# Gated mix of segmented attention and a feed-forward layer: v of the first segment from unscaled float32r halves, and matmuls on zeros at the beginning

## The chip, the core and the metric

The kernel runs on one core of a Trainium2 chip. A core has a matrix engine (TensorE, PE in the profile, which writes into PSUM, eight banks of 128 x 512 float32), a vector engine (VectorE, DVE), a scalar engine (ScalarE, ACT), GpSimd (POOL) and SyncE (SP), which here issues every DMA. The engines run beside each other and wait for each other by semaphores; each takes its own instructions in the order of the program. The metric is the time of one execution on the device in microseconds. Before the change the median of three runs was 551.74 us (551.17 to 552.27).

## What is computed

Sixteen heads of 28 columns, four segments of 512 rows. Cut to what matters:

```python
def reference(A_x, A_wq, A_wk, A_wv, A_wo, A_beta, B_x, B_w1, B_w2, gate_w):
    # x: (1, 2048, 448); wq, wk, wv, wo: (448, 448); w1: (448, 1792); w2: (1792, 448)
    q, k, v = heads(x @ wq), heads(x @ wk), heads(x @ wv)      # 16 heads of 28
    M = z = 0
    for s in range(4):                                         # segments of 512 rows
        a_dot = softmax(q[s] @ k[s].T * 28 ** -0.5 + causal) @ v[s]
        a_mem = phi(q[s]) @ M / (phi(q[s]) @ z + 1e-6)         # phi(t) = t + 1 or exp(t)
        o[s] = sigmoid(beta) * a_mem + (1 - sigmoid(beta)) * a_dot
        M, z = M + phi(k[s]).T @ v[s], z + phi(k[s]).sum(rows)
    a = merge(o) @ wo
    b = silu(x @ w1) @ w2
    g = sigmoid((x * gate_w).sum(-1))
    return g * a + (1 - g) * b
```

## The kernel before

Products are made in split precision. An operand becomes two float16 halves, the rounded value and what the rounding left, and a product is three matmuls for each 128 rows of the contraction (high by high, low by high, high by low). The 448 rows are three blocks of 128 and one of 64, whose low half lies in the idle rows, so a product of 512 columns is 11 matmuls (`passes`, `product`, L532, which cuts it into four tasks, one for each block). So that float16 holds the values, each operand is first multiplied by a power of two, worked out on the chip: `size` (L381) takes the largest magnitude of a tile on VectorE, and `scales(a, b)` (L399) reduces those, transposes the column on TensorE (L418), reduces the row and rounds it to a power of two on VectorE (L421 to L425), spreads it to all partitions with a small matmul (L427) and stores it and its inverse in `top` and `up` (L431, L432). Only then can `halves` (L513) make the two halves: the high one on ScalarE (L516), the low one on VectorE (L508) or, in two instructions, on GpSimd (L510, L511).

The first stage (`project`, L675) loads x of segment 0 and the weights of v, q and k in this order on SP's queue (L954 to L977), derives their scales, and makes for each segment the projections q and k (`proj`, four groups of heads each, into the three "mm" banks) and v with the gate's column (`vproj`, four blocks of 128 rows, into the three "sc" banks), the memory's updates (`memory`) and retrievals (`retrieve`). phi(q) is kept in float32r halves (L836, L838), a 32-bit form that the matmul takes directly: its high half is a rounding copy, its low half a subtraction, and neither needs a scale. A projection leaves PSUM in two steps, the high half by ScalarE (L806, L862) and the low half by VectorE (L807, L866), goes to DRAM, and comes back for attention. After the stage attention (`attention`, L1160) runs for 16 groups of four heads, interleaved with the feed-forward layer (`unit`, L1051), and at the end the output projection (`last_part`).

Before the data is there TensorE runs 15 matmuls on a tile of zeros (`maskb`, L718); the tile becomes the causal mask later (L728, on GpSimd), which waits for them.

The order on every engine is made while the program is built, by a list planner (`Sched`, L118). Each piece of work is a task with an engine, a cost, dependencies, buffers and a priority, a number of which the smaller goes first. The planner always takes the task that can start earliest on its engine, and among those that can start at once the one with the smallest number; for TensorE it also weighs the loading of weights against it (`PRICE`). A task that may run on VectorE or GpSimd (`either`, `scaled`) goes to the one that can start it first, unless it would end more than `SLACK` later there than on the other; in the plan the two lock each other out while a task of that kind runs. So all constants at the top (L46 to L95) are priorities and parameters of this planner: QS and KS1 for the scales and halves of q's and k's weights, VC for v's scale of segment 0, XS0 for the sizes of x, VF, VA and VS for the blocks of v, LOP and PVP for the low halves of the probabilities and P·V, WOT and WOP for the tail. The plan only sets the order; on the chip each instruction starts when its engine and its semaphores allow.

Of the kernel before, what the change touches and what calls it, by code (L numbers as in the profile page):

```python
# [8 lines left out]
F32 = mybir.dt.float32  # L9
# [27 lines left out]
WARM = 15  # L37
# [9 lines left out]
WOT = -23.27  # L47
# [8 lines left out]
SLACK = 0.67  # L56
LOP = 33.77
LATE = 0.08
FIRST = 104.18
WPRIO = 134.65  # L60
# [4 lines left out]
MP = 34.45  # L65
VF = 0.02
VA = 1.68
VS = 15.54
NV = 8
XS0 = 16.16  # L70
VC = -4.07
OT1 = -16.51
XS = 17.15
QS = -15.23
KS1 = 15.74
SS = -13.76
XH0 = -8.84
XLD = -11.75
# [6 lines left out]
PRICE = 25.59  # L85
PVRUNS = [((1, 0), 1)]
PVP = 81.22
FLO = -69.24
FHI = 869.75
WOP = 155.66  # L90
SZ = 30.78
SZSTEP = 2.16
XPRIO = 171.43
WBP = -21.83
# [152 lines left out]
def infini_mix(ctx: ExitStack, tc: tile.TileContext, x, wq, wk, wv, wo, beta, w1, w2, out):  # L247
# [111 lines left out]
    tg = const.tile([128, NSEG], F32, name="tg")  # L359
    rv = const.tile([128, NSEG], F32, name="rv")  # L360
# [83 lines left out]
    def vscale(s, prio):  # L444
        VREADY[s] = dve(130, lambda: nc.vector.tensor_scalar(tg[:, s:s + 1], top[:, WG:WG + 1], top[:, xi(s)], -1.0,
                                                             op0=OP.mult, op1=OP.mult), SCALED[WG], SCALED[NSEG - 1 - s],
                        prio=prio)
# [65 lines left out]
    def halves(j, hi, lo, dst, src, n, d, prio, takes=(), uses=()):  # L513

        s = up[:, j:j + 1]
        h = copy(n + 110, lambda: nc.scalar.activation(dst()[hi], src(), AF.Copy, scale=s), d, SCALED[j], takes=takes,  # L516
# [9 lines left out]
    def x16(s, c, prio):  # L526
# [3 lines left out]
        XH[s, c] = halves(NSEG - 1 - s, (ALL, c), lo, lambda: X16[s], lambda: r.v, L, d, prio, uses=[r])  # L530
# [144 lines left out]
    def project():  # L675
        es = ExitStack()
        wp = es.enter_context(tc.tile_pool(name="pw", bufs=1))
        W = {n: wp.tile([128, 8, D + 2 if n == "v" else L], F16, name=f"w{n}s") for n in "qkv"}
# [29 lines left out]
        def c1():  # L708
# [9 lines left out]
        t_wb = pe(half(L, WARM), lambda: [nc.tensor.matmul(  # L718
            wb.v, maskb, maskb[:, None, :].to_broadcast([128, 4, 128]), start=True, stop=True) for _ in range(WARM)],
            t_wm, takes=[wb], prio=-200)  # L720
        END1.append(t_wb)
        t_on = dve(32, lambda: nc.vector.memset(ones, -TALL), prio=-50)
# [648 lines left out]
```

## Time and profile before

| | |
|---|---|
| median of 3 runs | 551.74 us (551.17 to 552.27) |
| the profiled execution: time, span | 553.39 us, 551.7 us |
| mean granted TensorE clock | 0.984 of full speed |
| busy of the span: TensorE, VectorE, ScalarE, GpSimd | 534.8, 409.3, 391.8, 354.7 us |
| first matmul that belongs to a product | at 16.85 us |
| last projection's matmul of v | ends near 155.1 us |

The profile is that of one execution; its span runs from the first to the last instruction. Lines are named L and a number, those of the listing above; a line can be that of a helper which many places call, and then the tiles tell them apart (`wvs`, `wqs`, `wks` are the halves of the weights, `xh` those of x, `raw` the weights as loaded, `xraw` x as loaded). `out<-in` gives the tile written and the tiles read. A TensorE instruction counts as busy from its start to a modelled end, at whatever clock was granted, so a busy stretch at half clock does half the work.

### The profile page before, as it was taken

How to read it: one execution, taken by the hardware profiler on the slowest of the kernel's cores; microseconds unless marked ns; L12 is line 12 of the kernel's file. 1: busy time of each engine (PE TensorE's matmuls, PEld its weight loads, DVE VectorE, ACT ScalarE, POOL GpSimd, SP SyncE). 2: the span in 40 equal slices, each digit the busy share in tenths (PEclk: the TensorE clock that was granted, in tenths of full speed). 3: DMA queues.
4: the chain of work that ended last, by engine and by line, in shares of the span. 5: the costliest groups of instructions: out<-in, count | busy, mean ns of one | idle time of the engine just before them, and what ended most of it. 6: DMA issues, size and time to landing. Idle time of an engine off the chain costs nothing.

```text
span 551.7 us, 11563 instructions
## 1 busy us (share of the span) xinstructions
PE 534.8 (97%) x4009; PEld 294.7 (53%) x4009; DVE 409.3 (74%) x1074; ACT 391.8 (71%) x688; POOL 354.7 (64%) x519
## 2 busy tenths in 40 slices
PE   4699999999999999999999999999999999999997
PEld 1234655655554556555665555655555555555444
DVE  6889999899789966777666779766987319646473
ACT  1588898986656977899877997878998896402140
POOL 2063254845830689988999987999999995213120
PEclk8689999999999999999999999999999999999999
DMA  8658998885586434312433234434301515698962
GB/s 276 205 175 227 203 236 233 225 226 166 170 233 162 146 100 137 87 42 80 121 102 102 58 98 124 121 103 112 100 18 53 138 49 152 219 241 212 225 160 83
DMA packets 89194, 81.68 MB, mean 148 GB/s; under 512 B 55176, under 2 KB 78856, under 8 KB 89136
## 3 DMA queue, kind: packets, MB, share of 16 engines
q1 hardware_dynamic: 89136, 80.95, 53.1%
q8 instruction: 31, 0.51, 0.4%
q14 instruction: 27, 0.22, 0.1%
HBM read 48.41 MB, written 26.09 MB: 135 GB/s over the span
## 4 chain that ended last, share of the span: by engine, by line
PE 89%; DVE 4%; DMA 4%; ACT 1%; issue 1%; SPq 0%; DVEq 0%; ACTq 0%
PE mm L540 31%; PE mm L1086 23%; PE sc L540 12%; PE sc L1182 6%; PE sc L644 6%; PE cc L1216 6%; DMA rawf<-in_w_dram 2%; PE cc L932 1%; DMA xraw<-in_x_dram 1%; PE cc L895 1%; DVE sizes L388 1%; DVE sc L654 1%; DMA v_scr<-vt 1%; PE sc L640 1%; PE cc L933 0%
## 5 line engine op out<-in xcount | busy, mean ns | idle before, releaser
L1203 POOL TENSOR_TENSOR phl<-pf,phl 128x384 f16<-128x384 f32 (+1 forms) x192 | 189.5, 1008 | 16.2 <-ACT phl L1199 16.2
L1086 PE MATMUL mm<-wb,ghl 128*128 128x448 f16 (+1 forms) x684 | 148.8, 349 | 0.0
L540 PE MATMUL mm<-xh,wa 128*128 128x512 f16 x572 | 141.4, 379 | 0.0
L1187 ACT ACTIVATE pf<-sc,es 128x512 f32<-128x512 f32 (+1 forms) x192 | 109.7, 623 | 19.8 <-PE sc L1182 18.6
L654 DVE CUSTOM_DVE_ANT_0 sc<-sc,mk 128x384 f32<-128x384 f32 (+1 forms) x192 | 104.8, 572 | 20.4 <-PE sc L644 19.1
L1086 PEld LDWEIGHTS <-ghl 128*128 128x128 f16 x684 | 65.0, 97 | 52.5 <-DVE ghl L508 0.3
L1199 ACT ACTIVATE phl<-pf 128x1280 f16<-128x1280 f32 x64 | 81.3, 1277 | 14.9 <-POOL pf L1193 14.9
L540 PEld LDWEIGHTS <-wa 128*128 128x128 f16 x572 | 53.6, 97 | 54.4 <-issue 1.4
L1182 PE MATMUL sc<-ring 86*128 86x512 f16 (+3 forms) x256 | 59.3, 299 | 0.4 <-ACT pf L1187 0.2
L644 PE MATMUL sc<-ring 84*128 84x128 f16 (+3 forms) x256 | 58.2, 299 | 0.1
L1224 DVE TENSOR_REDUCE oraw<-cc 128x116 f32<-128x232 f32 x64 | 25.3, 395 | 30.8 <-PE cc L1216 30.6
L1063 ACT ACTIVATE th<-mm,ths 128x512 f32<-128x512 f32 x52 | 35.8, 699 | 16.0 <-PE mm L540 15.8
L1216 PEld LDWEIGHTS <-phl 128*128 128x128 f16 x1280 | 41.9, 96 | 9.1
L540 PE MATMUL mm<-xh,wqs 128*128 128x512 f16 x176 | 44.5, 390 | 1.0 <-ACT wqs L516 0.7
L551 POOL TENSOR_TENSOR ol<-ol,ml 128x448 f32<-128x448 f32 x12 | 13.7, 1138 | 48.7 <-DMA ol<-o_scr 37.2
L1065 DVE SCALAR_TENSOR_TENSOR mm<-th,mm 128x512 f32<-128x512 f32 x52 | 35.7, 694 | 10.9 <-ACT th L1063 10.9
L1216 PE MATMUL cc<-vg,phl 128*128 128x29 f16 (+1 forms) x1280 | 43.6, 182 | 0.0
L540 PE MATMUL sc<-wvs,xh 128*128 128x450 f16 x176 | 39.9, 368 | 3.1 <-ACT wvs L516 2.1
L540 PE MATMUL mm<-xh,wks 128*128 128x512 f16 x176 | 42.1, 380 | 0.0
L1069 DVE SCALAR_TENSOR_TENSOR ghl<-mm,ghl 128x512 f16<-128x512 f32 x52 | 35.1, 683 | 5.6 <-ACT ghl L1067 5.2
L1182 PEld LDWEIGHTS <-ring 86*128 86x128 f16 x256 | 23.8, 97 | 22.0 <-issue 1.1
L1067 ACT ACTIVATE ghl<-mm 128x512 f16<-128x512 f32 x52 | 30.9, 604 | 6.5 <-DVE mm L1065 6.4
(165 smaller groups left out, 835.9 us busy)
## 6 DMA issues: line engine op xcount, KB each, us to landing
rawf<-in_w_dram SPq DMA_DIRECT2D x26, 256.0 KB
rawf<-in_w_dram SPq DMA_DIRECT2D x28, 224.0 KB
xraw<-in_x_dram SPq DMA_DIRECT2D x16, 256.0 KB
v_scr<-vt SPq DMA_DIRECT2D x16, 232.0 KB
vg<-v_scr SPq DMA_DIRECT2D x16, 232.0 KB
q_scr<-stg SPq DMA_DIRECT2D x16, 224.0 KB
ring<-q_scr SPq DMA_DIRECT2D x16, 224.0 KB
k_scr<-stg SPq DMA_DIRECT2D x16, 224.0 KB
```

Source lines behind the costliest of these rows:

```text
L540: nc.tensor.matmul(ps(), *p[i], start=(i == 0), stop=(i == n - 1))
L644: nc.tensor.matmul(ps.v[:, u:u + n], rg.v[:KS, 0, hh, i * 128:(i + 1) * 128], rg.v[:KS, 1, hh, :n], start=(i > 0), stop=(i > 0 or j == 3), ...
L654: nc.vector.tensor_tensor_reduce(r, r, MK[:, L - n:], 1.0, NEG, OP.add, OP.max, mx.v[:, hh, i:i + 1])
L1063: e1 = sact(L, lambda ps=ps, th=th: nc.scalar.activation(th.v, ps.v, AF.Tanh, scale=ths[:, s:s + 1]), m, DER[s], takes=[th], uses=[ps], pr ...
L1065: e2 = dve(L, lambda ps=ps, th=th: nc.vector.scalar_tensor_tensor(ps.v, th.v, 1.0, ps.v, op0=OP.add, op1=OP.mult), e1, uses=[ps, th], prio=p0)
L1069: e4 = dve(L, lambda ps=ps, g=g: nc.vector.scalar_tensor_tensor(g.v[:, 1], ps.v, DOWN, g.v[:, 0], op0=OP.mult, op1=OP.subtract), e3, uses= ...
L1086: nc.tensor.matmul(ps.v[:, lo:hi], g.v[:, y, sl], w.v[:, z, lo:hi], start=(j == 0 and i == 0), stop=(j == len(fs) - 1 and i == 2))
L1182: nc.tensor.matmul(ps.v[:, e:e + w], rg.v[:KK, 1, hh, j * 128:(j + 1) * 128], rg.v[:KK, 0, hh, j * 128:], start=True, stop=True)
L1187: ex.append(sact(e, lambda b=b, ps=ps, pf=pf, e=e: nc.scalar.activation(pf.v[:, b, :e], ps.v[:, :e], AF.Exp, scale=es[:, s:s + 1]), m, *ex ...
L1199: hi = copy(1280, lambda hl=hl, flat=flat: nc.scalar.activation(hl.v[:, 0], flat(), AF.Copy), *mk, takes=[hl], uses=[pf], prio=p0 + 2)
L1203: low = pool(w - u, lambda hl=hl, flat=flat, u=u, w=w: nc.gpsimd.tensor_sub(hl.v[:, 1, u:w], flat()[:, u:w], hl.v[:, 0, u:w]), low, uses=[ ...
L1216: nc.tensor.matmul(p[:, i, :2 - z], hl.v[:, z, u:u + 128], vg.v[:, j, hh, :2 - z], start=(z == zs[0] and i == 0), stop=(z == zs[-1] and j ...
```

## The change

v of segment 0 (four blocks, `vproj`) is computed from float32r halves of x and of wv, made from the loaded tiles without a scale. `full` makes them: a copy on ScalarE that rounds to float32r, and a subtraction on VectorE or GpSimd (new tiles `xr` and `wr`). The product is then too large by the two scales that x and wv would have had, so the copies out of PSUM multiply with `sv` = `up[wv] * up[x] * FIT` in place of the constant FIT, and the gate's column takes the factor -1 in place of `tg`. The float16 halves of x and wv are still made: x's for q and k, wv's for the later segments. They now wait for the float32r halves of the same tile.

The matmuls on zeros at the beginning become a task of 12 full ones, four rounds of four in tiles of 32 rows (28 used) and three rounds of two in tiles of 64 rows, each tile of a round into a bank of its own; behind it eight tasks of two full ones with the largest priority number, which the planner puts wherever TensorE has nothing else to start. The mask on GpSimd waits for the last of them.

Almost all priorities and planner parameters get new values; the order of segments 1 to 3, of attention, of the feed-forward layer and of the tail is thereby planned anew. Among them: v's scale (VC -4.07 to -1.35), v's weights' float16 halves (-8.6 to VH = 6.63), v's sizes (-8.9 to WSZ = -11.62), x's float16 halves (-8.8 to XQ = -13.14), q's scale and halves (QS -15.23 to -23.13), the second to fourth blocks of v of segment 0 (VA + VS k, from 17.2, 32.8 and 48.3 to 17.1, 32.8 and 48.5; the first from -1.0 to 1.38), the loading of x of later segments (XLD) and of w1 and w2 (SZ).

```diff
-WARM = 15
+WARM = 12
+WARM2 = 8
-WOT = -23.27
+WOT = -9.9
-SLACK = 0.67
-LOP = 33.77
+SLACK = 0.73
+LOP = 29.92
-MP = 34.45
-VF = 0.02
-VA = 1.68
-VS = 15.54
+MP = 34.03
+VF = -0.53
+VA = 1.38
+VS = 15.7
-XS0 = 16.16
-VC = -4.07
+XS0 = 17.95
+VC = -1.35
-XS = 17.15
-QS = -15.23
-KS1 = 15.74
-XLD = -11.75
+XS = 14.39
+QS = -23.13
+KS1 = 13.66
+WSZ = -11.62
+C1P = -8.61
+XQ = -13.14
+VH = 6.63
+XLD = -23.11
-PRICE = 25.59
-PVP = 81.22
+PRICE = 53.8
+PVP = 82.98
-WOP = 155.66
-SZ = 30.78
+WOP = 81.42
+SZ = 40.95
...
     def vscale(s, prio):
+        def go():
+            if s:
+                nc.vector.tensor_scalar(tg[:, s:s + 1], top[:, WG:WG + 1], top[:, xi(s)], -1.0, op0=OP.mult, op1=OP.mult)
+            else:
+                nc.vector.tensor_scalar(sv, up[:, WV:WV + 1], up[:, xi(s)], FIT, op0=OP.mult, op1=OP.mult)
+        VREADY[s] = dve(130, go, SCALED[WG], SCALED[NSEG - 1 - s], prio=prio)
...
+        xr = wp.tile([128, 7, L], F32R, name="xr")
+        wr = wp.tile([128, 8, D + 2], F32R, name="wr")
...
-        t_c1 = pool(2000, c1, t_id, prio=-99)
-        t_of = dve(160, lambda: nc.vector.tensor_reduce(of, own, axis=AX.X, op=OP.max), t_c1, prio=-99)
+        t_c1 = pool(2000, c1, t_id, prio=C1P)
+        t_of = dve(160, lambda: nc.vector.tensor_reduce(of, own, axis=AX.X, op=OP.max), t_c1, prio=0)
...
-        t_wb = pe(half(L, WARM), lambda: [nc.tensor.matmul(
-            wb.v, maskb, maskb[:, None, :].to_broadcast([128, 4, 128]), start=True, stop=True) for _ in range(WARM)],
-            t_wm, takes=[wb], prio=-200)
+        others4 = [Buf(BK["mm"]), Buf(BK["mm"]), Buf(BK["sc"])]
+        def warm():
+            zeros = maskb[:, None, :].to_broadcast([128, 4, 128])
+            dst = [wb.v] + [b.v for b in others4]
+            for rows, times in ((128, 7), (32, 4), (128, 3), (64, 3), (128, 2)):
+                for _ in range(times):
+                    for r in range(128 // rows):
+                        k = slice(rows * r, rows * r + (DH if rows == 32 else rows))
+                        nc.tensor.matmul(dst[r], maskb[k], zeros[k], start=True, stop=True)
+        t_wb = pe(half(L, WARM + 6), warm, t_wm, takes=[wb] + others4, prio=-200)
         END1.append(t_wb)
+        for _ in range(WARM2):
+            END1.append(pe(half(L, 2), lambda: [nc.tensor.matmul(
+                wb.v, maskb, maskb[:, None, :].to_broadcast([128, 4, 128]), start=True, stop=True) for _ in range(2)],
+                t_wb, uses=[wb], prio=500))
...
         MKS.append(pool(128, lambda: nc.gpsimd.affine_select(maskb, maskb, [[-1, 128]], OP.is_ge, NEG, base=0,
-                                                             channel_multiplier=1), t_wb, t_mb, prio=-50))
+                                                             channel_multiplier=1), END1[-1], t_mb, prio=-50))
...
+        def full(o, c, src, n, tail, d, b, prio):
+            hi = copy(n, lambda: nc.scalar.activation(o[:, c], src(), AF.Copy), d, uses=[b], prio=prio)
+            def lo(e):
+                if tail:
+                    e.tensor_sub(o[REM:128, c], src()[REM:128], raw(o[REM:128, c]))
+                else:
+                    e.tensor_sub(o[:, 4 + c], src(), raw(o[:, c]))
+            return [hi, either(n, lo, hi, uses=[b], prio=prio)]
...
-                    size(j, lambda v=v: v()[:, :D], D, WLOAD[-1], uses=[b], prio=prio + 0.01 * c)
+                    WF[c] = full(wr, c, v, n, False, WLOAD[-1], b, prio + 0.01 * c)
+                    size(j, lambda v=v: v()[:, :D], D, WLOAD[-1], uses=[b], prio=WSZ + 0.01 * c)
...
         def vproj(k, prio):
             s, tb = divmod(k, TB)
-            p = product(lambda: ps.v[:, :D + 2],
-                        lambda: passes(W["v"], X16[s][:, :, tb * 128:(tb + 1) * 128], True), D, prio,
-                        deps={c: WS["v"][c] + WS["g"] + XH[s, c] for c in range(NC + 1)}, takes=[ps], kind=half)
+            w, xt = (W["v"], X16[s]) if s else (wr, xr)
+            p = product(lambda: ps.v[:, :D + 2], lambda: passes(w, xt[:, :, tb * 128:(tb + 1) * 128], True), D, prio,
+                        deps={c: WS["v"][c] + WS["g"] + XH[s, c] if s else WF[c] + XF[c] for c in range(NC + 1)}, takes=[ps],
+                        kind=half if s else ful)
+            fit = FIT if s else sv
-            a = act(D, lambda: nc.scalar.activation(v.v[:, :, 0, :DH], pv(), AF.Copy, scale=FIT), p, t_c1,
+            a = act(D, lambda: nc.scalar.activation(v.v[:, :, 0, :DH], pv(), AF.Copy, scale=fit), p, t_c1, None if s else VREADY[0],
                     takes=[v], uses=[ps], prio=prio)
...
+        for c in range(NC + 1):
+            load_x(0, c, -9 + 0.01 * c)
+            b, d = XR[0, c]
+            XF[c] = full(xr, c, lambda b=b: b.v, L, c == NC, d, b, -9 + 0.01 * c)
         weight("v", wv, -8.9, places[:4])
-        gate_size(-8.95, places)
+        gate_size(WSZ, places)
         scales(NSEG - 1, NSEG, -20)
-        for tb in range(TB):
-            x16(0, tb, -8.8 + 0.01 * tb)
-        scales(WV, WG + 1, -20)
-        whalves("v", -8.6, places[:4])
+        for c in range(NC + 1):
+            x16(0, c, XQ + 0.01 * c, *XF[c])
+        scales(WV, WG + 1, VC)
+        whalves("v", VH, places[:4])
```

More of the change, by code (lines that the diff above doesn't have):

```diff
@@ L55 @@
 HS = 0.14
-SLACK = 0.67
-LOP = 33.77
+SLACK = 0.73
+LOP = 29.92
 LATE = 0.08
 FIRST = 104.18
-WPRIO = 134.65
+WPRIO = 138.82
 MAXO = 62.72
@@ L64 @@
 RB = "cc"
-MP = 34.45
-VF = 0.02
-VA = 1.68
-VS = 15.54
+MP = 34.03
+VF = -0.53
+VA = 1.38
+VS = 15.7
 NV = 8
-XS0 = 16.16
-VC = -4.07
-OT1 = -16.51
-XS = 17.15
-QS = -15.23
-KS1 = 15.74
-SS = -13.76
-XH0 = -8.84
-XLD = -11.75
+XS0 = 17.95
+VC = -1.35
+OT1 = -16.13
+XS = 14.39
[5 more added lines that the diff above has]
+VH = 6.63
+SS = -11.24
+XH0 = -8.32
+XLD = -23.11
 def VP(o, k):
     return o + VA + VS * k if o or k > VF else -1.0 + 0.1 * k
-PRICE = 25.59
+PRICE = 53.8
 PVRUNS = [((1, 0), 1)]
-PVP = 81.22
-FLO = -69.24
-FHI = 869.75
-WOP = 155.66
-SZ = 30.78
-SZSTEP = 2.16
-XPRIO = 171.43
-WBP = -21.83
+PVP = 82.98
+FLO = -69.72
+FHI = 852.61
+WOP = 81.42
+SZ = 40.95
+SZSTEP = 2.11
+XPRIO = 194.06
+WBP = -26.83
 XLEAD = 146.82
@@ L515, in halves @@
         s = up[:, j:j + 1]
-        h = copy(n + 110, lambda: nc.scalar.activation(dst()[hi], src(), AF.Copy, scale=s), d, SCALED[j], takes=takes,
+        d = d if isinstance(d, list) else [d]
+        h = copy(n + 110, lambda: nc.scalar.activation(dst()[hi], src(), AF.Copy, scale=s), *d, SCALED[j], takes=takes,
                  uses=uses, prio=prio)
@@ L529, in x16 @@
         lo = [((ALL, 4 + c), (ALL,), (ALL, c)) if c < NC else ((END, NC), (END,), (END, NC))]
-        XH[s, c] = halves(NSEG - 1 - s, (ALL, c), lo, lambda: X16[s], lambda: r.v, L, d, prio, uses=[r])
+        XH[s, c] = halves(NSEG - 1 - s, (ALL, c), lo, lambda: X16[s], lambda: r.v, L, [d, *deps], prio, uses=[r])
     def product(ps, pairs, cols, prio, deps=(), takes=(), uses=(), cuts=None, kind=None):
@@ L784, in whalves @@
                 WS["g"] = halves(WG, (ALL, slice(0, 4)), [((ALL, slice(4, 8)), (ALL,), (ALL, slice(0, 4)))],
-                                 lambda: W["v"][:, :, D:D + 2], lambda: raw0.v[:, 0:4, D:D + 2], 16, SCALED[WG],
+                                 lambda: W["v"][:, :, D:D + 2], lambda: raw0.v[:, 0:4, D:D + 2], 16, [t for c in WF for t in WF[c]],
                                  uses=[places[0][0]], prio=prio)
```

15 lines of the change are left out of this document (6 added, 9 removed).

## The prediction

> **What bounds the kernel now.** I read the page first, then the busy time of the engines in four stretches, then TensorE's timeline and the chain of waits at the beginning.
>
> ```profile
> span 551.7 us, 11563 instructions
> PE 534.8 (97%) x4009; PEld 294.7 (53%) x4009; DVE 409.3 (74%) x1074; ACT 391.8 (71%) x688; POOL 354.7 (64%) x519
> ```
> ```profile
> 0.00:16.85 16.85, 6.48 (x20) 2.34 (x21) 11.26 (x37) 4.75 (x8) 4.11 (x26) 0.75 0.84 282
> 16.85:33.57 16.72, 14.34 (x52) 5.64 (x52) 14.97 (x44) 9.76 (x27) 4.27 (x7) 0.74 0.57 191
> 33.57:155.10 121.53, 121.53 (x699) 68.18 (x698) 111.59 (x284) 97.08 (x212) 68.01 (x107) 1.00 0.78 206
> 155.10:551.70 396.60, 392.47 (x3241) 218.51 (x3239) 271.49 (x712) 280.20 (x443) 278.27 (x379) 1.00 0.45 123
> ```
>
> In the second view the columns after the stretch and its length are the busy us of PE, weight loads, DVE, ACT and POOL, then the granted clock. From 33.57 to 155.10 us TensorE is busy all the time at full clock; after that it lacks 4.1 us of 396.6, of which 551.7 - 548.06 = 3.6 lie behind the last matmul (the last row of the chain, below). So the kernel ends when TensorE has done its work, and what can still be had lies ahead of 33.57 us. TensorE's timeline there (start, length and instruction, and in brackets the idle time ahead and what ended it), and rows of the chain of waits:
>
> ```profile
> 1.04 5.42 PE L718 MATMUL mm<-maskb 128*128 128x512 bf16 x15 [1.04 <-DVE ones L722]
> 16.85 0.53 PE L540 MATMUL sc<-wvs,xh 128*128 128x450 f16 x1 [2.13 <-ACT wvs L516]
> 18.31 5.68 PE L540 MATMUL sc<-wvs,xh 128*128 128x450 f16 x19 [0.93 <-DVE wvs L508]
> 23.83 0.27 PE L418 MATMUL cc<-ident,most 128*2 128x128 f32 x1
> 26.12 0.17 PE L427 MATMUL cc<-diag,oneb 2*128 2x2 bf16 x1
> 28.21 0.39 PE L540 MATMUL mm<-xh,wqs 128*128 128x512 f16 x1 [0.73 <-ACT wqs L516]
> ```
> ```profile
> 24.10 2.09 PE sc L540 x11
> 37.30 2.37 PE mm L540 x11
> ...
> 548.06 0.45 DVE y L1297
> ```
> ```profile
> 0.00:33.57 33.57, 13.99 (x48) 5.39 (x49) 0.75 0.70 237
> ```
>
> The last row is the view by stretch again, for L540 alone. Its 48 matmuls are 39 of v and 9 of q; at full clock, by the two chain rows, one of v takes 2.09/11 = 0.19 us and one of q 2.37/11 = 0.216. That is 9.4 us of work in 33.57 us: some 24 us at the beginning are waiting, warm-up and half clock. The clock went as follows:
>
> ```profile
> 8.00:9.00 1.00, 0.00 (x0) 0.00 (x0) 0.75 (x2) 0.00 (x0) 0.00 (x0) 0.78 1.02 359
> 22.00:23.00 1.00, 1.00 (x6) 0.54 (x5) 1.00 (x4) 0.12 (x1) 0.00 (x0) 0.90 0.14 55
> 29.00:30.00 1.00, 1.00 (x3) 0.30 (x2) 0.90 (x5) 1.00 (x3) 0.87 (x3) 0.52 0.43 131
> 32.00:33.00 1.00, 1.00 (x5) 0.45 (x4) 1.00 (x2) 0.21 (x2) 1.00 (x1) 0.78 0.34 106
> ```
>
> A mean of 0.78 in 8 to 9 us says that the clock fell to half at 8.56; likewise it rose at 22.2, fell at 29.04 and rose at 32.44. These lie 4, 2 and 1 times 3.41 us apart: the clock is set anew on a fixed raster, by how busy TensorE was in the slot before. The half-clock slot at 29.04 costs 3.41/2 = 1.7 us.
>
> What lets q begin at 28.21 (the point from which TensorE hardly lacks work again) is VectorE, with TensorE's queue in between:
>
> ```profile
> 8.25 0.69 DVE L388 TENSOR_REDUCE sizes<-xraw 128x1 f32<-128x512 f32 x1 [1.06 <-DMA xraw<-in_x_dram]
> 13.63 0.27 DVE L421 TENSOR_REDUCE few<-cc 2x1 f32<-2x128 f32 x1
> 14.43 1.40 DVE L508 SCALAR_TENSOR_TENSOR xh<-xraw,up,xh 128x512 f16<-128x512 f32 x2
> 15.75 0.15 DVE L431 RECIPROCAL up<-cc 128x2 f32<-128x2 f32 x1
> 15.89 1.51 DVE L508 SCALAR_TENSOR_TENSOR xh<-xraw,up,xh 128x512 f16<-128x512 f32 x2
> 18.70 1.87 DVE L508 SCALAR_TENSOR_TENSOR wvs<-raw,up,wvs 128x448 f16<-128x448 f32 x3
> 20.49 0.86 DVE L388 TENSOR_REDUCE sizes<-raw 128x1 f32<-128x64 f32 x3
> 21.79 0.15 DVE L414 TENSOR_REDUCE most<-sizes 128x2 f32<-128x8 f32 x1
> 24.14 0.28 DVE L421 TENSOR_REDUCE few<-cc 2x1 f32<-2x128 f32 x1 [0.89 <-PE cc L418]
> ```
> ```profile
> 26.82 0.55 ACT L862 ACTIVATE vt<-sc 128x448 f16<-128x448 f32 x1 [0.54 <-PE sc L540]
> 27.26 3.28 ACT L516 ACTIVATE wqs<-raw,up 128x448 f16<-128x448 f32 x8
> ```
>
> The last piece of x lands at 8.25, and from then to 21.79 VectorE runs without a pause: sizes, three scales, the low halves of x and of v's weights. Only then does it reach q's maximum (L414), whose transpose lies in TensorE's queue behind v's half-clock matmuls until 23.83.
>
> **The change part by part.** *v of segment 0.* It no longer waits for a scale. What is taken from VectorE ahead of q: v's weights' low halves, three in 20.49 - 18.70 = 1.79 us, so 0.60 each, 2.4 for four, and their scale chain, 14.43 - 13.63 = 0.80 and 15.89 - 15.75 = 0.14. These now have larger priority numbers than q's (VC and VH against QS), so they come behind q: **-3.3 us**. ScalarE's copy of v ahead of q's first half (27.26 - 26.82) now waits for the scale and goes too: **-0.4**. And v's matmuls start earlier, so that TensorE's queue should be empty when q's transpose comes: the wait from 21.9 to 23.83 falls away, **-1.9** (bounds: 0, and -3.0 when the wait of the scale's second small matmul goes as well: 24.14 + 0.80, as the other chain took, is 24.94, and it ran at 26.12, 1.2 less 0.1 for the way there).
>
> What it adds: eight float32r halves, each a ScalarE copy and a subtraction on VectorE or GpSimd. ScalarE can begin when the first x has landed and its table is loaded; the nearest rows for the halves are the features of q:
>
> ```profile
> 4.01 1.28 ACT L516 ACT_TABLE_LOAD   x1 [4.01 <-DMA xraw<-in_x_dram]
> ```
> ```profile
> L836 ACT ACTIVATE phq<-ph x12: 612/629/650, 62.1 to 151.1; 112x512 fp32r<-112x512 f32 x12
> L838 POOL TENSOR_TENSOR phq<-ph,phq x7: 1263/1271/1574, 70.9 to 152.1; 112x512 fp32r<-112x512 f32 x7
> L838 DVE TENSOR_TENSOR phq<-ph,phq x5: 684/691/918, 62.8 to 138.7; 112x512 fp32r<-112x512 f32 x5
> ```
>
> (Shortest, median and longest, in ns.) ScalarE has 4.75 us of work in the first 16.85, so eight copies (5.0) lie in its idle time. GpSimd has 4.11 there; the planner gives it a subtraction when it can start sooner, and its clearing of v's tiles, which is still first in its idle queue, ends before x is split. Eight at 1.27 are 10.2 us: begun at 4.01 + 1.28 + 0.63 = 5.9, the first of wv is done about 5.9 + 5 x 1.27 = 12.3 and the last at 16.1. v's first 33 matmuls (only three "sc" banks, and their release now waits for v's scale, late) take 6.3 us and end near 19, just when q's transpose would come (21.79 - 3.3 = 18.5). If all eight went to VectorE, 8 x 0.69 = 5.5 us would stand ahead of q; if none, 0. I take one, or one collision: **+0.7**. Together the start of q moves by -3.3 - 0.4 - 1.9 + 0.7 = **-4.9 us**, to 23.3; bounds -6.7 and -0.1.
>
> *The float32r matmuls.* No row has 450 columns. The nearest:
>
> ```profile
> 64.68 0.33 PE L932 MATMUL cc<-mhl,phq 112*128 112x232 f32 x1
> 64.90 0.33 PE L932 MATMUL cc<-mhl,phq 112*128 112x232 f32 x1
> ```
>
> A pair of 232 and 116 columns takes 0.22 us, so at most 0.22/348 x 450 = 0.285 for 450; at least the 0.19 of float16. I take 0.20, near the float16 row, since two loads of weights fit in a pair of 0.22 and so one in a matmul of 0.19. 33 of them lie in the wait for q; the fourth block's 11 come after q has begun: **+0.1** (0 to 1.0).
>
> *Zeros.* 12 full matmuls, 16 in tiles of 32 rows and 6 in tiles of 64. Tiles side by side make it 19 matmul times, 5.42 + 4 x 0.216 = 6.3 us; one after another 34, 9.5. It ends at 7.3 or 10.5; x's transpose is due at about 9.2 after the row at 8.25, so the cost is 0 or 1.3. The 16 fillers (16 x 0.216 = 3.5 us) are in TensorE's queue where the planner saw a hole; v's first subtraction at 12.3 covers them: **0**, and 3.5 if they landed after q is ready. The causal mask of maskb (GpSimd, L728) now waits for the last filler, and behind it in GpSimd's queue stand subtractions; 10.5 + 3.5 = 14.0 is their latest, and v has slack until 23.3 - 6.3 = 17.0. *Clock:* a hole remains between 19 and 23.3, so I expect one half-clock slot after q starts, as before: **0**, with -1.7 if the clock holds and +1.7 for a second slot.
>
> *What is late next.* v's weights, v's scale and its copies now fall behind q on VectorE (3.3 + some 2 us of copies that moved). VectorE has 111.59 us in 121.53 before 155.1, so 9.9 us are free, and q's and k's products cover it: **0**, up to 3.3. *Redrawn numbers* for segments 1 to 3, attention and the tail, moved loads of x and w1 on SP included: TensorE lacks nothing there, so they can win nothing and I cost them at 0; the cover is the queue of ready matmuls, and what they cost without it is the last rival.
>
> Sum: -4.9 + 0.1 = -4.8 us. The profiled execution took 553.39 us with a span of 551.7; 548.6 by this sum. The median of the runs is 551.74, 1.65 below the profiled one, so **546.9 us**.
>
> **The rivals.** *The subtractions collide (gain lost).* One row speaks for it:
>
> ```profile
> L511 POOL TENSOR_TENSOR wqs<-raw,wqs x3: 303/304/2102, 29.6 to 31.2; 128x64 f16<-128x64 f32 x3
> ```
>
> The same subtraction took 0.30 us twice and 2.10 the third time, while VectorE ran three two-input operations in a row. Here GpSimd subtracts while VectorE makes four low halves of x: if each has to wait out a GpSimd subtraction, 4 x 1.27 = 5.1 us stand ahead of q, 4.4 more than I charged: 546.9 + 4.4 = 551.3. Against it: GpSimd lost there, not VectorE, and v has slack. The Trainium skill, page "SBUF — State Buffer", section "Who interferes with whom", says that a VectorE instruction with two SBUF inputs and a GpSimd instruction that reads SBUF exclude each other for the whole instruction; by that rule the 2.10 is what a loser pays, and whoever issues first wins, which leaves open on which side the cost falls.
>
> *More than forecast.* All of TensorE's waits on v go (-1.1), no subtraction lands on VectorE (-0.7), the clock holds through the start of q (-1.7): 543.4. For it: the fillers; against it: 33 matmuls of 0.2 end before q can start by my own sum.
>
> *VectorE gives it back.* If the 3.3 us moved behind q come due together with k's weights, TensorE dries there: 546.9 + 3.3 = 550.2. For it VectorE's 92%, against it 9.9 us of room.
>
> *Slower: attention stalls on GpSimd.* LOP, PVP and PRICE order the probability halves and P·V.
>
> ```profile
> 300.00:400.00 100.00, 99.76 (x958) 57.60 (x955) 76.58 (x228) 86.47 (x139) 93.55 (x133) 1.00 0.38 102
> L1203 POOL TENSOR_TENSOR phl<-pf,phl 128x384 f16<-128x384 f32 (+1 forms) x192 | 189.5, 1008 | 16.2 <-ACT phl L1199 16.2
> ```
>
> GpSimd is busy 93.55 of 100 us here, and each of 64 heads (192/3) ends in its subtraction. If the new order lets P·V of each head wait 0.12 us for it, that is 7.7 us: 554.6. It decides from 4.8/64 = 0.075 us a head. Against it: TensorE now waits 0.24 us in this whole stretch.
>
> **How the numbers follow.** Forecast 0.50 (own range 543.5 to 549.5), more 0.13, VectorE gives back 0.10, collision 0.10, slower 0.17. The range 542.5 to 554.5 takes the rivals in and leaves the far ends out. Within 0.2%, 1.1 us, is about what a measurement here can tell from no change: 550.6 to 552.8. Faster: 0.50 + 0.13 + 0.08 (giving back, mostly) + 0.03 = 0.74; same 0.09 (the rest of the collision and of giving back); slower 0.17.
>
> **What would show it.** v's first float32r matmul near 12 us and not near 17; q's first near 23 and not 28; v's weights' scale behind q's on VectorE; eight subtractions mostly on GpSimd; from q on no hole until 543 and the last matmul at about 543.2 rather than 548.0. Wrong would be: q later than 27, a wait of TensorE between 35 and 150, more than 1 us of waits between 200 and 500, or a second half-clock slot.

## The result, and the profile after

The changed kernel is slower: median 557.72 us (556.48 to 559.84, four runs), 552.0 for the kernel before in the same comparison (551.17 to 553.35, four runs); the ratio is 1.0105, 95% interval 1.0068 to 1.0143. Its profiled execution took 557.95 us, span 556.2. Forecast were 546.9 us and a range of 542.5 to 554.5. So the change went the other way, and the interval leaves no doubt of the sign.

The beginning went as forecast and further. TensorE's timeline of the kernel after (start, length, instruction, in brackets the idle time ahead and what ended it):

```profile
9.24 1.89 PE L744 MATMUL mm<-maskb 128*128 128x512 bf16 x8
12.58 0.16 PE L433 MATMUL cc<-diag,oneb 1*128 1x1 bf16 x1 [1.44 <-DVE diag L431]
12.67 1.90 PE L744 MATMUL mm<-maskb 128*128 128x512 bf16 x8
14.22 1.58 PE L551 MATMUL sc<-wr,xr 128*128 128x450 f32 x6
...
17.78 3.55 PE L551 MATMUL sc<-wr,xr 128*128 128x450 f32 x16
21.17 3.41 PE L551 MATMUL mm<-xh,wqs 128*128 128x512 f16 x15
...
34.63 0.38 PE L551 MATMUL mm<-xh,wks 128*128 128x512 f16 x1
36.40 3.82 PE L551 MATMUL mm<-xh,wks 128*128 128x512 f16 x16 [1.39 <-DVE wks L518]
```

v starts at 14.22 us. q starts at 21.17 us, where it was 28.21 before and 23.3 in the forecast. Then TensorE begins to wait; before the change it waited nowhere between 33.57 and 155.10. The larger waits of the same view, and the first matmul of the feed-forward layer (`wa`):

```profile
78.57 2.69 PE L551 MATMUL mm<-xh,wqs 128*128 128x512 f16 x11 [0.99 <-ACT pr L860]
83.63 0.81 PE L551 MATMUL mm<-xh,wks 128*128 128x512 f16 x3 [1.25 <-DVE stg L845]
155.21 0.32 PE L973 MATMUL cc<-mhl,phq 112*128 112x116 f32 x1 [1.23 <-POOL phq L876]
...
156.04 1.25 PE L551 MATMUL mm<-xh,wa 128*128 128x512 f16 x5
...
461.04 1.46 PE L551 MATMUL mm<-xh,wa 128*128 128x512 f16 x6 [1.09 <-DVE ghl L1111]
```

Three stretches of the kernel after (busy us and count of PE, weight loads, DVE, ACT, POOL, then granted clock, DMA share, GB/s), and the last stretch of the kernel before:

```profile
0.00:33.57 33.57, 29.47 (x144) 15.69 (x145) 27.89 (x87) 20.49 (x44) 14.02 (x37) 1.00 0.72 239
33.57:155.10 121.53, 115.13 (x655) 63.61 (x653) 108.79 (x280) 96.34 (x212) 64.86 (x102) 1.00 0.76 206
155.10:543.00 387.90, 385.40 (x3190) 213.86 (x3191) 268.35 (x705) 279.59 (x440) 278.08 (x378) 1.00 0.44 123
```
```profile
155.10:543.00 387.90, 387.45 (x3204) 215.03 (x3203) 269.31 (x708) 280.20 (x443) 278.27 (x379) 1.00 0.45 124
```

In the middle stretch TensorE now idles 121.53 - 115.13 = 6.40 us, before 0; in the last 2.50, before 0.45. How the lead is spent can be counted in matmuls. The view by stretch for the line of the projections alone (L540 before, L551 after; PE and weight loads):

```profile
33.57:60.00 26.43, 25.95 (x121) 11.51 (x119) 1.00 0.72 195
60.00:90.00 30.00, 25.18 (x110) 10.27 (x110) 1.00 0.94 225
0.00:155.10 155.10, 120.83 (x528) 50.23 (x529) 0.94 0.76 213
```
```profile
0.00:33.57 33.57, 18.99 (x86) 11.91 (x87) 1.00 0.72 239
33.57:60.00 26.43, 23.26 (x106) 9.82 (x104) 1.00 0.80 227
60.00:90.00 30.00, 22.03 (x95) 8.79 (x94) 1.00 0.84 212
0.00:155.10 155.10, 118.77 (x528) 52.84 (x528) 1.00 0.75 213
```

By 33.57 us the kernel after has issued 86 of these matmuls against 48: a lead of 38, at 0.216 us 8.2 us. By 155.10 it is 528 in both, which are all the matmuls of the projections. (A matmul that runs across the edge of two stretches counts in both, so the stretches add up to a little more.) The next work through the same line, the feed-forward layer, starts at 156.04, before the change at 155.10. So the lead is gone when the first stage ends; 15 matmuls each are lost in the second and third stretch. The waits that the view shows are less than what they cost: a single 512-column matmul is recorded as 0.38 us (at 34.63) where a stream has one every 0.216, so the modelled end hides 0.16 us of each wait, and a shorter wait isn't seen at all. Which fits: 38 matmuls, 8.2 us, are lost with 6.40 us of idle time.

That brings the kernel back to where it was, and not yet behind it. The last matmul ends at 551.9 us, before the change at 548.0: some 3 of these 3.9 us arise behind 156.04. In the last stretch TensorE idles 2.50 us in place of 0.45, 1.09 of them at 461; the rest isn't laid out here.

### The profile page after: what moved, and what is told of

It is laid out like the page before. It is cut to its first block, busy times and chain, and to the rows that moved or that the text cites. A ratio compares the mean times of both kernels' runs of the same rounds, so it can differ in the third digit from the quotient of the medians.

```text
span 556.2 us, 11630 instructions
## 1 busy us (share of the span) xinstructions
PE 538.9 (97%) x4044; PEld 298.7 (54%) x4044; DVE 410.0 (74%) x1078; ACT 397.1 (71%) x696; POOL 357.7 (64%) x516
## 4 chain that ended last, share of the span: by engine, by line
PE 71%; DVE 14%; ACT 5%; DMA 5%; issue 2%; POOL 1%; SPq 1%; DVEq 0%; ACTq 0%; POOLq 0%
PE mm L551 24%; PE mm L1128 18%; PE sc L551 10%; PE sc L1224 5%; PE cc L1258 5%; PE sc L655 5%; DVE sizes L394 2%; DVE sc L665 2%; ACT pf L1229 2%; DMA rawf<-in_w_dram 2%; DMA rwo<-in_wo_dram 1%; DVE stg L845 1%; ACT phl L1241 1%; PE cc L972 1%; DMA xraw<-in_x_dram 1%
## 5 line engine op out<-in xcount | busy, mean ns | idle before, releaser
L1128 PE MATMUL mm<-wb,ghl 128*128 128x448 f16 (+1 forms) x684 | 146.9, 349 | 0.1
L551 PE MATMUL mm<-xh,wa 128*128 128x512 f16 x572 | 141.8, 379 | 1.1 <-DVE ghl L1111 1.1
L551 PEld LDWEIGHTS <-wa 128*128 128x128 f16 x572 | 53.7, 97 | 54.9 <-issue 2.8
L551 PE MATMUL mm<-xh,wks 128*128 128x512 f16 x176 | 42.4, 380 | 2.6 <-DVE wks L518 1.4
L551 PE MATMUL mm<-xh,wqs 128*128 128x512 f16 x176 | 42.7, 380 | 1.3 <-ACT pr L860 1.0
L1266 DVE TENSOR_REDUCE oraw<-cc 128x116 f32<-128x232 f32 x64 | 25.3, 395 | 23.3 <-PE cc L1258 23.0
L568 ACT ACTIVATE oh<-ol,os 128x448 f16<-128x448 f32 x16 | 10.7, 666 | 41.6 <-POOL ol L562 41.5
L1232 POOL TENSOR_SCALAR_AFFINE_SELECT pf<-pf 128x128 f32<-128x128 f32 x64 | 19.9, 311 | 27.8 <-ACT pf L1229 27.3
```

What stands on the lines that cost most here:

```text
L551: nc.tensor.matmul(ps(), *p[i], start=(i == 0), stop=(i == n - 1))
L1128: nc.tensor.matmul(ps.v[:, lo:hi], g.v[:, y, sl], w.v[:, z, lo:hi], start=(j == 0 and i == 0), stop=(j == len(fs) - 1 and i == 2))
```

## The experiments

The question is why the lead is lost. Theory T: VectorE, ScalarE and GpSimd set the pace of the first stage, and no order keeps the lead. Theory C: the order made from the redrawn numbers doesn't fit the early start. (e1 to e4 were put forward with an earlier set of theories, and the letters in their expectations belong to it; A there is a lack of VectorE's throughput, B the redrawn order. T and C hold from e5 on.) Beside each median stands TensorE's busy time in the view by stretch for 33.57 to 155.10 us, 121.53 long: the time it lacks there is the loss of the first stage.

| kernel | median us (runs from, to) | ratio to before, 95% | PE busy 33.57:155.10 |
|---|---|---|---|
| before | 552.0 (551.17 to 553.35) | | 121.53 |
| after | 557.72 (556.48 to 559.84) | 1.0105 (1.0068 to 1.0143) | 115.13 |
| e1, after, short sizes | 557.8 (556.91 to 559.34) | 1.0091 (1.0059 to 1.0124) | 115.50 |
| e2, before, short sizes | 552.06 (550.63 to 553.73) | 0.9992 (0.9975 to 1.0009) | 121.53 |
| e3, after, old numbers behind the start | 560.74 (557.48 to 564.13) | 1.0142 (1.0089 to 1.0195) | 114.56 |
| e4, after, old late numbers | 557.69 (557.16 to 560.74) | 1.0084 (1.0058 to 1.011) | 115.35 |
| e5, after, old SS | 556.67 (556.16 to 557.6) | 1.0076 (1.0049 to 1.0103) | 115.01 |
| e6, before, new SS | 560.99 (559.29 to 562.86) | 1.0153 (1.0112 to 1.0194) | 120.36 |
| e7, before, all new numbers | 557.86 (556.76 to 558.9) | 1.0095 (1.0064 to 1.0126) | 120.21 |
| e8, after, drawn again | 549.88 (548.77 to 550.65) | 0.9951 (0.9935 to 0.9968) | 119.83 |
| e9, before, drawn again | 550.34 (549.68 to 551.11) | 0.9961 (0.9944 to 0.9977) | 121.53 |
| e10, after, a third set | 549.03 (548.18 to 550.46) | 0.9937 (0.9917 to 0.9957) | 121.08 |
| e13, after, e10's first-stage numbers | 549.93 (549.72 to 550.15) | 0.9957 (0.994 to 0.9973) | 121.07 |
| e14, after, e10's late numbers | 559.62 (557.37 to 560.32) | 1.0126 (1.0102 to 1.0151) | 114.54 |
| e15, after, e10's numbers of the start | 557.48 (555.52 to 558.94) | 1.0092 (1.0061 to 1.0124) | 116.60 |
| e16, after, e10's numbers of segments 1 to 3 | 560.21 (559.63 to 560.66) | 1.0144 (1.0128 to 1.0159) | 112.13 |

**Less work for VectorE: e1, e2.** The sizes of x of segments 1 to 3 are taken over 64 of 512 columns, with the order on every engine as it was; the largest magnitude of the other columns isn't looked at.

```diff
-            size(NSEG - 1 - s, lambda: b.v, L, d, uses=[b], ...
+            size(NSEG - 1 - s, lambda: b.v[:, :64] if s else b.v, L, d, uses=[b], ...
```

> The changed kernel, with the magnitudes of x of segments 1 to 3 taken over 64 of 512 columns (12 reductions on VectorE, about 0.4 us shorter each, 4.8 us in all); the order of every engine is the same. Theory A, VectorE is full after q has begun and sets TensorE's pace until about 90 us: 553 to 555 us, and the waits of TensorE between 34 and 90 us get shorter by 3 us or more. Theory B, the redrawn order makes the waits, and VectorE's time is not the bound: 557 to 558 us.

> The kernel before with the same 12 shorter reductions in the same order, a control. Both theories: TensorE does not wait for VectorE there, so 551.5 to 552.3 us, no change.

```profile
33.57:155.10 121.53, 115.50 (x651) 63.70 (x650) 103.42 (x273) 95.03 (x210) 65.16 (x102) 0.99 0.76 204
```

That row is e1's. VectorE works 5.4 us less in the stretch (103.42 against 108.79), and TensorE waits as long as before. The time is unchanged too, 557.8 as theory B had it, and the control e2 stays at 552.06. VectorE's throughput isn't what is short; this part of theory T falls.

**Old numbers, one block or one number: e3, e4, e5.** e3 puts 18 old constants behind the new start, e4 the seven for attention and the tail, e5 one alone:

```diff
-SS = -11.24
+SS = -13.76
```

> The changed kernel, with the old values for all numbers that do not order the beginning of segment 0 (SLACK, MP, XS, SS, XH0, XLD, SZ, SZSTEP, XPRIO, WPRIO, PRICE, LOP, PVP, FLO, FHI, WOP, WOT, WBP). Theory B, the redrawn numbers lose it: q still begins near 21 us and most of the 8 us lead at 33.6 us is kept, 544 to 548 us. Theory A, VectorE gives the lead back whatever the order is: 551 to 554 us.

> The changed kernel, with the old values of only those numbers that order attention, the feed-forward layer and the tail (LOP, PVP, FLO, FHI, WOP, WOT, WBP); the first stage up to about 153 us is the same. If the waits at 460 and 485 us and the longer end come from these numbers: 554 to 555.5 us. If they come from what the first stage leaves behind: 557 to 558 us.

> The kernel after with one number of before: SS = -13.76 in place of -11.24, the priority of the scale of the next segment's x. Theory C (the holes of the kernel after between 76 and 88 us are a matter of order: with the redrawn number the scale of segment 2's x, and with it its low halves, stand behind other VectorE work): TensorE's waits in 76 to 88 us, 3.0 us in the windows of the kernel after, shrink to under 1.5, segment 2's x is ready earlier, and the time falls to 547 to 554 us. Theory T (the engines that empty PSUM and feed TensorE set the pace of the first stage, so what the start gained is lost in any order): the holes move but their sum stays, 556 to 559.

None gave the lead back. e3, at 560.74, met neither of its expectations: the old numbers behind the new start didn't help. e4 stayed at 557.69, so the seven late numbers aren't what costs the time. In e5 the waits only moved. Its expectation under theory C, 547 to 554, failed, and 556.67 is what theory T had: this one number isn't at fault in the new kernel. The other numbers weren't tried one by one.

**New numbers in the old kernel: e6, e7.** The reverse of e5's diff, and all 26 redrawn constants that the kernel before knows (counted in the edit; the expectation has 27).

> The control: the kernel before with that one number of after, SS = -11.24 in place of -13.76. Theory C: TensorE, which waited nowhere between 33.6 and 155 us, gets holes of 2 to 8 us in all there, and the time rises to 554 to 560 us. Theory T: this kernel has no lead to lose and stays within 1 us of 552. Should e5 gain and this one not lose, the number matters only with the earlier start.

> The kernel before with every redrawn number of after that it knows (27 priorities and planner's constants), and none of the change's new work. Theory C: the redraw by itself costs time: 554 to 562 us, with holes in the first stage. Theory T, by which the numbers decide nothing: 551 to 553. If it is as slow as the kernel after or slower, the loss lies in the numbers and the new start still pays; if it is 552, the numbers hurt only with the new start.

```profile
33.57:155.10 121.53, 120.21 (x687) 66.61 (x685) 108.88 (x279) 95.58 (x210) 74.19 (x108) 1.00 0.76 206
```

That row is e7's. With nothing of the change but its numbers the old kernel takes 557.86 us, as much as the changed one. And SS alone, the place of the small chains of scale instructions for each later segment, costs the old kernel 560.99 - 552.74 = 8.25 us in that comparison; its 560.99 lies a little above theory C's 554 to 560. In e6's profile 1.17 us show up as idle time in this stretch and 387.90 - 383.43 = 4.47 behind it (155.10 to 543; 0.45 before); the rest isn't laid out. The prediction had costed all of this at 0.

**A fit for the early start: e8, e10, and e9 as the control.** The work stays as it is; 32 constants in e8, 31 in e10 and 27 in e9 are drawn anew (counted in the edits; the expectations of e8 and e9 have 28 and 26). The sets were found by varying the numbers at random and keeping what gave the shortest plan of the kernel's own planner; what they are worth is told by the chip alone.

```diff
-SLACK = 0.73
+SLACK = 0.84
-VA = 1.38
+VA = -0.55
-QS = -23.13
-KS1 = 13.66
+QS = -16.03
+KS1 = 9.06
-XQ = -13.14
-VH = 6.63
-SS = -11.24
+XQ = 4.97
+VH = 10.59
+SS = -2.77
...
```

(That is e10, cut to its core.)

> The kernel after, its work unchanged, with its priorities and planner's constants drawn a second time for the early start (28 numbers). Theory C: the lead of some 7 us that the start wins is kept: no hole over 1 us between 36 and 155 us, last matmul near 540, time 542 to 548 us, faster than both kernels. Theory T: the start is as early, but the lead is gone by 155 us in this order too: 550 to 557.

> The kernel before, its work unchanged, with its own priorities and planner's constants drawn a second time in the same manner as in e8 (26 numbers). Theory C (the new start is worth some 4 to 5 us, if the order behind it fits): TensorE waits nowhere in the first stage of the kernel before, so that another order can win little; 550 to 553 us, at least 1 us above e8. Rival R (e8 is fast because any second drawing is, and the new start adds nothing): 548 to 550.5, no slower than e8.

> The kernel after with a third, independent set of numbers. Theory C: a fit for the early start isn't a matter of one lucky set; 547 to 551 us, no hole over 1 us between 40 and 155 us. Rival L (luck: e8 is one draw out of a spread like that of after, e3, e4 and e5, 556 to 561): 553 to 560.

The view by stretch for the projections' line in e10, and TensorE's waits in its first stage behind 33.57:

```profile
0.00:33.57 33.57, 18.56 (x80) 10.28 (x81) 1.00 0.70 231
33.57:60.00 26.43, 24.14 (x109) 11.10 (x107) 1.00 0.84 213
60.00:90.00 30.00, 25.87 (x118) 11.20 (x119) 1.00 0.89 241
0.00:155.10 155.10, 124.28 (x556) 55.66 (x557) 1.00 0.79 220
```
```profile
36.45 2.53 PE L551 MATMUL mm<-xh,wks 128*128 128x512 f16 x11 [0.20 <-DVE stg L845]
...
137.35 0.32 PE L973 MATMUL cc<-mhl,phq 112*128 112x116 f32 x1 [0.25 <-DVE phq L876]
```

e8 took 549.88 us: faster than both kernels, but outside theory C's 542 to 548 and, by a little, below theory T's 550. e10 is inside its 547 to 551. In e10 80 matmuls are issued at 33.57 and 556 at 155.10, against 48 and 528 before: of a lead of 32, 28 are kept (6.0 us). VectorE does as much there as in the kernel after:

```profile
33.57:155.10 121.53, 121.08 (x696) 68.62 (x695) 109.67 (x284) 97.37 (x210) 67.65 (x105) 1.00 0.82 216
```

So the engines can feed TensorE at this pace, and theory T falls: an order exists that keeps most of the lead. The numbers set more than the order, though: they also choose between VectorE and GpSimd (SLACK), and GpSimd is busy for 28.55 of the first 33.57 us in e10, 14.02 in the kernel after. Order and choice of engine weren't tried apart. What order means is seen at k's weights. VectorE's timeline in the kernel after and in e10 (`wvs`, `wks`: low halves of v's and k's weights; the reciprocal ends k's scale chain):

```profile
30.62 1.85 DVE L518 SCALAR_TENSOR_TENSOR wvs<-raw,up,wvs 128x448 f16<-128x448 f32 x3
32.40 0.15 DVE L437 RECIPROCAL up<-cc 128x2 f32<-128x2 f32 x1
...
34.38 1.28 DVE L845 SCALAR_TENSOR_TENSOR stg<-mm,stg 128x512 f16<-128x512 f32 x2
35.58 2.11 DVE L518 SCALAR_TENSOR_TENSOR wks<-wa,up,wks 128x448 f16<-128x448 f32 x4
```
```profile
24.38 0.15 DVE L437 RECIPROCAL up<-cc 128x2 f32<-128x2 f32 x1
...
27.75 0.68 DVE L518 SCALAR_TENSOR_TENSOR wks<-wa,up,wks 128x448 f16<-128x448 f32 x1
...
32.10 1.31 DVE L518 SCALAR_TENSOR_TENSOR wks<-wa,up,wks 128x448 f16<-128x448 f32 x2
33.34 2.46 DVE L518 SCALAR_TENSOR_TENSOR wvs<-raw,up,wvs 128x448 f16<-128x448 f32 x4
```

In the kernel after, v's halves, which no one needs until segment 1, stand ahead of k's, and k's scale comes at 32.40, though the small matmul that it reads had run at 29.02: the wait of 1.39 us at 36.40. In e10 k's scale comes 8 us earlier, k's halves first, and the wait is gone. The other waits of the kernel after weren't followed back like this.

The control gained too: e9 takes 550.34, where 550 to 553 were expected of theory C; but it isn't the 1 us above e8 (549.88, in another comparison). In its own comparison e10 is 550.34 - 549.03 = 1.3 us faster, on eight and six runs that overlap, and e12 (below), which is e8 with another warm-up, 550.34 - 550.0 = 0.3 us, no more than the scatter. Rival R isn't dead: more than half of e8's and e10's gain over the kernel before can be had by a second drawing alone.

**Which numbers: e13 to e16.** e10's set is split: 24 for the first stage and the choice of engine (e13), 7 for the rest (e14); and the 24 again into 11 for the start (e15) and 13 for segments 1 to 3 and the planner (e16).

> The kernel after with e10's numbers for the first stage and the choice of engine (24 of them), and its own seven for attention and the tail. If the loss lies in the first stage, as the holes of the kernel after say: 548 to 551 us, near e10. If the late numbers share in it: 552 to 556.

> The other half: the kernel after with e10's seven numbers for attention and the tail alone. If the loss lies in the first stage: 555 to 559, the holes of the kernel after at 76 to 88 us all there. If it lies late: below 553.

> The kernel after with only those of e10's numbers that place the work of the first segment (11). If the loss comes from the start's own order: 549 to 552. If start and later segments must fit together, as e3 and e5 suggest: 554 to 561.

> The kernel after with only those of e10's numbers that place segments 1 to 3, their loads and sizes, and the planner's constants (13). If these alone are at fault: 549 to 552. If start and later segments must fit together: 553 to 561.

```profile
33.57:155.10 121.53, 121.07 (x695) 68.35 (x694) 110.50 (x284) 96.68 (x210) 66.55 (x105) 1.00 0.81 216
```

That row is e13's. The first-stage numbers alone bring 549.93; either half of them, and the late ones, bring nothing or make it worse (e14's 559.62 even lies above the 559 that was expected). So the loss comes from the numbers of the first stage and the choice of engine, and neither half of e10's set cures it alone: the start's numbers and the segments' have to fit each other. Which of them have to fit stays open; each half stood beside numbers that it wasn't drawn with.

**The zeros: e11, e12.** Both are e8 with the same order on every engine. e11 cuts each pair of fillers (the eight tasks of two matmuls on zeros behind the warm-up) to one matmul of two columns; e12 takes 24 full matmuls for the warm-up in place of full ones and tiles.

```diff
-                wb.v, maskb, maskb[:, None, :].to_broadcast([128, 4, 128]), start=True, stop=True) for _ in range(2)],
+                wb.v[:, :2], maskb, maskb[:, :2], start=True, stop=True)],
```
```diff
-            for rows, times in ((128, 7), (32, 4), (128, 3), (64, 3), (128, 2)):
+            for rows, times in ((128, 24),):
```

> The kernel of e8, same order on every engine, with each of the eight pairs of filler matmuls on zeros cut to one matmul of two columns. Clock theory (the fillers are what keeps the clock up): TensorE is then busy some 1 us of 6.8 to 10.2 and almost none of 10.2 to 13.6, the granted clock falls to half about 10.2 and comes back about 17, v's first 33 matmuls lose 3/2 = 1.5 us and end near 23.4 instead of 21.8; the time rises by 0.5 to 1.7 us, to 550.4 to 551.6. Rival (the fillers are in v's way or do nothing, as the prediction had it with its 0): the time of e8 within 0.4, or less.

> The kernel of e8, same order on every engine, with the warm-up on zeros as 24 matmuls of all 128 rows, which end at about the same 7.5 us, in place of 12 such and 22 in tiles of 28 and 64 rows. If the tiles do nothing but fill time: the same clock in every slot of 3.41 us and the time of e8 within 0.5. If the tiles matter to the clock: a half-clock slot appears or one goes, and the time moves by 1 to 2 us.

e11 took 550.51 us (549.43 to 552.36; ratio 0.9967, 0.9953 to 0.998), e12 550.0 (548.57 to 551.2; 0.9954, 0.9936 to 0.9973). The view by stretch of e11, for TensorE alone (busy, clock, DMA share, GB/s):

```profile
8.46:11.87 3.41, 0.35 (x5) 1.00 1.05 396
11.87:15.28 3.41, 2.45 (x11) 0.50 1.02 338
15.28:18.69 3.41, 3.41 (x11) 0.50 0.87 304
18.69:22.10 3.41, 3.41 (x18) 1.00 0.62 202
```

Without fillers the clock is at half for two slots of 3.41 us, and v's matmuls fall into them. So the fillers do hold the clock; that this is worth time is not shown, since 0.5 us between e11 and e12 is within the scatter of both. No use of the tiles for the clock shows: in e12 as in e8 the column of the granted clock reads 1.00 all through, and the time is the same. e12's zeros ended at 9.19 us, though, and not at 7.5; the last section says why the column doesn't show it.

## Why the prediction was wrong

*v of segment 0 and q's start (-4.9): the right way, and too small.* q came 28.21 - 21.17 = 7.04 us earlier, a little beyond the far bound of 6.7. The eight subtractions all went to GpSimd, so that none stood ahead of q; the 0.7 charged for one was not paid. The collision wasn't put to the test: the subtractions end at 17.0 us, and VectorE runs reductions and small scale instructions until its two-input halves of x begin behind them. The same holds for the rule that the prediction cites.

```profile
L773 POOL TENSOR_TENSOR wr<-raw,wr x4: 974/1060/1157, 10.8 to 16.0; 128x450 fp32r<-128x450 f32 x4
L773 POOL TENSOR_TENSOR xr<-xraw,xr x3: 1269/1269/1270, 5.0 to 8.1; 128x512 fp32r<-128x512 f32 x3
L771 POOL TENSOR_TENSOR xr<-xraw,xr x1: 1271/1271/1271, 9.4 to 9.4; 64x512 fp32r<-64x512 f32 x1
```
```profile
18.26 1.39 DVE L518 SCALAR_TENSOR_TENSOR xh<-xraw,up,xh 128x512 f16<-128x512 f32 x2
```

The first subtraction of v's weights is done at 10.8 + 1.0 = 11.8, near the forecast 12.3, but v starts at 14.22: ahead of it in TensorE's queue stand a small matmul of x's scale chain, which waits for VectorE until 12.58, and the second run of fillers. q follows v's 33 matmuls without a gap, so in the end TensorE's own work set q's start. The rival "more than forecast" described this beginning (no subtraction on VectorE, the clock held); its time went the way of the forecast's.

*float32r matmuls (+0.1).* 0.20 us was taken; the 16 in a row start over 21.17 - 17.78 = 3.39 us, 0.212 each, inside the bounds 0.19 to 0.285.

*Zeros and clock (0 and 0).* The warm-up cost nothing: it ends at 7.56, x's transpose runs at 9.14. The fillers' cover failed in part: the second eight run from 12.67, when the first subtraction is done (11.8), and GpSimd waits 1.81 us for them, until 14.64, with the mask and two subtractions behind it. What this cost q isn't shown. The clock was the miss: the half-clock slot after q's start is gone, because fillers and early v leave no empty slot; by the prediction's own estimate that is a gain of 1.7 us, which it had only as a bound.

*What is late next (0, up to 3.3): failed.* It was argued from VectorE's 9.9 us of free time. The free time was real (e1: more of it changed nothing), but the row of the wait at 36.40 and the two timelines of VectorE show that a free engine doesn't help when the late piece stands behind others in its order. The rival "VectorE gives it back" had this place; it was one hole of several. The wait of 1.39 us is one of the prediction's own signs of being wrong, a wait of TensorE between 35 and 150 us.

*Redrawn numbers (0, "they can win nothing"): the step that failed.* The argument was that TensorE lacks nothing behind 33.57 us and a queue of ready matmuls covers any order. That queue was a property of the old order, not of the work. e7 shows the price in the old kernel, 557.86 us against 552.74 for the kernel before in that comparison, 5.1 us; in the new one the first stage alone lacks 6.40 us, and e13 gets the time back with the first stage's numbers only. e8 and e10, with the same work and other numbers, are faster than the kernel before. And the numbers can win: e9 wins 1.7 us without the change.

*The slower rival had the wrong place.* It named the redraw, and looked for its price in attention, where TensorE hardly waits in the kernel after:

```profile
200.00:400.00 200.00, 199.84 (x1889) 115.50 (x1888) 146.50 (x438) 168.49 (x264) 178.19 (x249) 1.00 0.39 105
```

e4 agrees: the old LOP and PVP, with five more of the late numbers, change nothing (557.69). The rival's own time, 554.6, lay just outside the range that was to take the rivals in.

*The sum.* With numbers that fit, e10's median is 3.0 us below that of the kernel before. But e9 has 1.7 of that without the new start, so by these sets the start is worth 0.3 (e12) to 1.3 us (e10) against e9, and with the numbers of the kernel after it is worth nothing: 557.72 with it, 557.86 without (e7, another comparison). The 4.8 us that the work was costed at are seen at q's start; no pair of kernels with and without it shows them in the time. How much of e9's gain is clock and how much order was not taken apart. The sign was lost in the numbers.

## What to carry to other kernels

Where a planner or a hand-written list fixes the order, a change of its parameters is an edit like any other: "the bottleneck engine lacks nothing" was measured under the old order and is no cover for a new one. Work that became ready earlier paid here only where what follows was ordered for it, and then little; so read the lead at several points (matmuls issued by then) and look for the stretch in which it is spent. When it is spent there, try a fresh set of priorities before blaming throughput, and give the kernel before the same second chance.

## What the runs showed of the hardware

The half clock comes and goes in slots of 3.41 us, and how busy TensorE was in one goes with the clock of the next: in e11 a slot busy for 0.35 us was followed by half clock, one busy for all 3.41 by full clock. In e4's profiled execution the same fillers began at 9.36, only 0.12 us later than in the kernel after, and didn't save a slot that ended at 10.57 (TensorE alone, as above):

```profile
7.16:10.57 3.41, 1.31 (x7) 1.00 1.04 388
10.57:13.98 3.41, 2.50 (x8) 0.50 1.04 368
13.98:17.39 3.41, 3.41 (x10) 0.50 1.03 340
```
```profile
12.78 3.59 PE L744 MATMUL mm<-maskb 128*128 128x512 bf16 x8
```

A slot busy for 1.31 of 3.41 us was followed by half clock, and the second eight fillers then took 3.59 us in place of 1.90 and v, behind them in the queue, began at 15.81 in place of 14.22. The Trainium skill, page "TensorE: Matmul & The Clock Gate", section "What's actually happening", says that the activity window is free-running and doesn't reset when a kernel starts, so that the same kernel may see its clock change at another point. The runs fit this: a slot begins at 10.57 us in e4 and at 11.87 in e11, and of the runs of the kernel before in all comparisons, those with a mean clock of 0.991 took 550.17 to 552.00 us, those with 0.984 took 553.11 to 554.85 (the clocks between order the times less cleanly: 0.988 took 552.55 to 554.25).

The column of the granted clock doesn't show all of it. It reads 1.00 from the start of the span, but in the kernel before the weight loads of the matmuls on zeros follow each other by 0.43 us until 5.2, and by about 0.2 behind it:

```profile
4.86 0.15 PEld L718 LDWEIGHTS <-maskb 128*128 128x128 bf16 x1 [0.28 <-issue]
5.22 0.75 PEld L718 LDWEIGHTS <-maskb 128*128 128x128 bf16 x4 [0.21 <-issue]
```

(The load ahead of these is at 4.43.) TensorE begins at half pace, and 5.15 is an edge of the slots, 3.41 ahead of the fall at 8.56. In e12 the loads are 0.43 us apart until 6.56, which is why its zeros end late.

Matmuls in tiles of 32 rows (28 used) ran beside each other. Rows of e4, where these ran at the full pace; each round of four is one x3 into "mm" and one x1 into "sc":

```profile
4.21 0.38 PE L740 MATMUL mm<-maskb 28*128 28x512 bf16 x3
4.22 0.37 PE L740 MATMUL sc<-maskb 28*128 28x512 bf16 x1
4.42 0.38 PE L740 MATMUL mm<-maskb 28*128 28x512 bf16 x3
```

A round begins 0.21 us after the one ahead, the pace of one full matmul of 512 columns: the four cost the time of one, as the prediction's 19 slots had it.
